# Moving the gate products ahead of the pair products in an RWKV-5 attention that feeds a mixture of experts

## The chip, the core and the metric

The kernel runs on one core of a Trainium2 chip. The metric is device time in microseconds (us) of one execution of the whole program, attention and experts together. A core has five engines that run on their own and wait for each other through semaphores: TensorE (PE in the profile; PEld is its row of weight loads, which overlap the products), VectorE (DVE), ScalarE (ACT), GpSimd (POOL) and SyncE (SP, which here only issues transfers).

## The reference, cut to what matters

```
batch, n_heads, seq, head_dim = (4, 8, 768, 48)
for t in range(S):
    kt, vt, rt = (k[:, :, t], v[:, :, t], r[:, :, t])
    cur = np.einsum('bhd,bhe->bhde', u[None] * kt, vt)
    y[:, :, t] = np.einsum('bhd,bhde->bhe', rt, state + cur)
    state = w[None, :, :, None] * state + np.einsum('bhd,bhe->bhde', kt, vt)
...
logits = x @ w_gate          # x: y as 3072 rows (tokens) of 384
# each token goes to one of 8 experts, best logits first, at most 384 tokens to an expert
h = np.maximum(x[mask] @ w1[e], 0.0)
out[mask] = h @ w2[e]
```

The gate's product, `x @ w_gate`, is what the change moves. The logits decide which tokens an expert takes, and the experts' two products come after that.

## The kernel before

The attention is class `Mild`. It cuts the sequence into 24 units of 128 steps of one batch: unit n is chunk n // 4 of batch n % 4 (N = 24, B = 4, C = 6). The order of all instructions is written out by hand, and each engine takes its own in that order. `run` makes one round for each unit, in a software pipeline: in round n, unit n + 2 is turned (transposed), unit n + 1 gets its pair products, and unit n its outputs. On TensorE a round from n = 3 on is this:

- `turn(n + 2)`: four transposes of the keys into `kT_ps` and four of the receptances into `rT_ps` (L458).
- `rows((n - 1,), "few")` (L685): four transposes of the finished unit n - 1 into `x_ps` (L595). ScalarE copies that out to `xr` (L604), and SP sends it to the token table in memory. This stands in rounds 1 to 20.
- `keep(n - 1)` (L695), in rounds up to n = 4 only: the state's products into `kv_ps` (L524).
- `pairs(n + 1)` (L697): 16 products of 48 rows into `g_ps` (L505). VectorE then copies the lower triangle from `g_ps` into `AT` with a mask, in two instructions (L512).
- In a round with a gate only, `gate(n // B - 1, ...)` (L705): 16 products into `lg_ps` (L575), four for each of four units n - 4 to n - 1, with the weights `wgp`. ScalarE copies them to `lg` (L580). These rounds are n = 4, 8, 12, 16 and 20 (`full`); a sixth gate comes after the last round and is not touched.
- `outputs(n)` (L711): eight products from the states (L545, `y_ps<-rT,states`), the eight of `keep(n)` (L524), and eight from `AT` (L545, `y_ps<-AT,vts`). After a gate a transpose of `lg` into `lt_ps` ends the round (L585), which ScalarE copies to the logits `LG` (L586). ScalarE then copies `y_ps` to `x` (L564).

What matters around the change is the buffer of the `few` tag. `x_ps` (L591), `lg_ps` (L571) and `lt_ps` (L584) all come from it, and its pool has one buffer. So a gate's first product waits until ScalarE's copy at L604 has read the `x_ps` before it. The `wgp` of the gate comes by two transfers that SP issues in round 2 (L404). `g_ps` has one buffer too, which VectorE's masked copy of the round before must have read.

ScalarE's share of a gate round is: the copy of `kT_ps` (L475), `xr` (L604), four diagonals of `AT` (L495), `lg` (L580), four more diagonals, `LG` (L586) and `x` (L564). VectorE's is: `rT` (L477), the masked copies (L512), and the state's sum (L529), beside the tables and the early steps of the assignment. In rounds 17 to 23 the assignment of an early expert is woven in (L1152 to L1270, products L1167, L1203, L1218).

After round 23 the last logits go into the assignment search, on VectorE for the most part, while TensorE runs the early expert. Then the eight experts follow, for which TensorE is busy nearly without a break.

Of the kernel before, what the change touches and what calls it, by code (L numbers as in the profile page):

```python
# [274 lines left out]
class Mild:  # L275
# [343 lines left out]
    def run(self, step):  # L619
        N, B, C, walk = self.N, self.B, self.C, self.walk  # L620
        self.live = {n: {} for n in range(N)}
        self.start()
        u_ps = self.spread_u()
        self.again_one(0, 0)
        k0 = self.keys_turned(0, True)
        self.again_one(0, 1)
        self.idle(2, "g_ps")
        r0 = self.r_turned(0)
        self.copy_u(u_ps)
        self.own(0)  # L630
        self.scaled(0, "k", k0, "pieces")
        self.scaled(0, "r", r0, "pieces")
        self.table(self.WK, "k")
        self.again_one(1, 0)
        self.table(self.WR, "r")
        self.again_one(1, 1)
        self.idle(2, "g_ps")
        k1 = self.keys_turned(1, True, walk.ps, "few")
        wk_ps = self.wk_turned()
        r1 = self.r_turned(1, walk.ps, "counts")  # L640
        self.wk_table(wk_ps)
        self.scaled(1, "k", k1, self.WK)
        self.own_sum(0)
        self.diagonal(0, (0,))
        self.again_one(2, 0)
        self.diagonal(0, (1,))
        self.again_one(2, 1)
        self.scaled(1, "r", r1, self.WR)
        self.own(1)
        self.keys(0)  # L650
        self.own_sum(1)
        nc, AB = self.nc, self.ones8
        nc.vector.tensor_mul(self.chunk, AB[:, 0, :, 1, 8], AB[:, 0, :, 1, 8])
        self.pairs(0)
        self.diagonal(1)
        self.own(2)
        chores = walk.constants()
        for n in range(N):
            self.load(n + 5, "kr")
            self.load(n + 4, "v")  # L660
            if n == 2:
                self.gate_weights()
            soon, split, full = n <= B, 0 < n < 3, n >= B and n % B == 0
            halves = ((0,), (1,)) if split or full else ((0, 1), ())
            if n == 0:
                self.turn(2, True)
                self.own_sum(2)
                self.idle(3, "y_ps")
                self.pairs(1)
                self.keys(1)  # L670
            else:
                step(n, "first")
                if not soon and n + 3 < N:
                    self.again(n + 3)
                if n == 2:
                    self.own_sum(n + 2)
                if split:
                    self.keep(n - 1)
                    self.pairs(n + 1)
                if n + 2 < N:  # L680
                    if n != 2 and n + 3 < N:
                        self.own_sum(n + 2)
                    self.turn(n + 2, between=lambda: step(n, "turning"))
                if n <= N - B:
                    self.rows((n - 1,), "few")  # L685
            if soon:
                self.again_one(n + 3, 0)
            if n + 2 < N:
                self.diagonal(n + 2, halves[0])
            if soon:  # L690
                self.again_one(n + 3, 1)
            if n > 2:
                step(n, "turned")
                if n <= B:
                    self.keep(n - 1)  # L695
                if n + 1 < N:
                    self.pairs(n + 1, lambda: step(n, "products"))  # L697
                step(n, "paired")
            if n + 3 < N:
                self.keys(n + 3)  # L700
                self.own(n + 3)
                if n == 1:
                    self.keys(2)
            if full:
                self.gate(n // B - 1, range(B))  # L705
                if n + 2 < N:
                    self.diagonal(n + 2, halves[1])
            if n == N - 1:
                rows = self.rows_turned((N - 4, N - 3), "g_ps", lambda: step(n, "rows"))
                self.rows_out((N - 4, N - 3), rows)  # L710
            self.outputs(n, lambda: step(n, "states"), (lambda: self.logits(n // B - 1)) if full else (lambda: None))  # L711
            if split:
                self.diagonal(n + 2, halves[1])
            if n == N - 4:
                self.own_sum(N - 1)
            step(n, "last")
            if n == 13:
                walk.guess_most(self.LG[:, 0:3 * B, :], AX.XY)
            if n == 14:
                walk.guess(walk.ps.tile([128, 128], F32, name="most_ps", tag="few"), self.ident)  # L720
            if n == N // 2 + 1:
                for _ in chores:
                    pass
                self.test()
            if n > 2:
                for _ in range(6):
                    next(chores, None)
        self.gate(C - 1, range(B - 1))
        one = self.rows_turned((N - 2,), "kT_ps")
        self.gate(C - 1, [B - 1])  # L730
        last = self.rows_turned((N - 1,), "g_ps")
        self.logits(C - 1)
        return one, last
# [1285 lines left out]
```

## Time and profile before

| | us |
|---|---|
| median of 3 runs | 393.32 (393.11 to 393.7) |
| the profiled execution's own time | 393.36 |
| its span, first to last instruction | 391.6 |
| rounds 4 to 20 in it, about | 30 to 113 |
| last logits copied, the search begins, about | 126.8 |

Times in the rows are us from the span's start. A row of the timeline gives start, length, engine, source line, operation, output<-inputs, shape and count, and in brackets how long the engine was idle before it and what ended that; "issue" there means that no wait which the profile shows did. TensorE's fp32 products appear twice each, so the 16 of a gate read x32. The span is 1.8 us shorter than that execution's time, and the execution lies within 0.04 us of the median.

### The profile page before, as it was taken

What the parts mean: (1) busy time and instruction counts of PE and PEld (TensorE: products, weight loads), DVE (VectorE), ACT (ScalarE), POOL (GpSimd) and SP (SyncE); (2) the same over time, 40 slices, a digit from 0 to 9 for tenths busy, and PEclk for the clock granted to TensorE, in tenths of its full rate; (3) what the DMA queues carried; (4) which work ended last, traced back from release to release, by engine and by line L of the source; (5) the groups of instructions that cost most, each with busy time, mean ns of one, the idle gap of its engine ahead of it and who ended that gap; (6) DMA issues with size and microseconds to landing.
All of it is one profiled execution on the core that took longest, in us unless ns stands there. A gap on an engine that the chain in (4) does not pass through costs nothing. (4 is left out here: it accounts for less than half of the span.)

```text
span 391.6 us, 9858 instructions
## 1 busy us (share of the span) xinstructions
PE 377.2 (96%) x3777; PEld 306.2 (78%) x3777; DVE 281.4 (72%) x959; ACT 169.3 (43%) x452; POOL 141.2 (36%) x173
## 2 busy tenths in 40 slices
PE   8899999999999999999999999999999999999992
PEld 7677888888877866687578899558657889989991
DVE  6755777586885788985949949888378976994530
ACT  4997989888883311312222242121222234234220
POOL 7878887767732022032122021203203212070020
PEclk9999999999999999999999999999999999999997
DMA  9999999988692164651560560109209264280010
GB/s 121 160 180 174 210 189 201 174 171 157 129 338 82 43 241 181 195 190 42 164 238 28 168 251 20 41 5 345 77 20 338 85 231 173 52 329 24 2 62 27
DMA packets 95335, 57.35 MB, mean 146 GB/s; under 512 B 77232, under 2 KB 89520, under 8 KB 95280
## 3 DMA queue, kind: packets, MB, share of 16 engines
q1 hardware_dynamic: 91936, 47.21, 48.0%
q0 software_dynamic: 3104, 9.44, 7.0%
q8 instruction: 31, 0.51, 0.6%
q14 instruction: 24, 0.20, 0.2%
q10 hardware_dynamic: 240, 0.00, 0.0%
HBM read 47.20 MB, written 9.44 MB: 145 GB/s over the span
## 5 line engine op out<-in xcount | busy, mean ns | idle before, releaser
L1624 PE MATMUL h_ps<-xT,w 128*128 128x384 f32 (+1 forms) x264 | 72.6, 427 | 0.0
L495 ACT ACTIVATE AT<-ident,dd 128x128 f32<-128x128 f32 x192 | 59.6, 392 | 2.2 <-DVE dd L448 2.1
L1624 PEld LDWEIGHTS h_ps<-xT,w 128*128 128x128 f32 x264 | 42.0, 191 | 19.6 <-issue 2.2
L1518 POOL DMA_INDIRECT xg<-x_rows,tok x22 | 22.5, 1021 | 92.4 <-PE h_ps L1624 23.7
L1750 POOL DMA_INDIRECT out_dram<-o_all,to x16 | 20.8, 1299 | 85.3 <-DVE o_all L1738 22.2
L1627 ACT ACTIVATE hid<-h_ps 128x384 f32<-128x384 f32 (+1 forms) x40 | 17.9, 449 | 54.2 <-PE h_ps L1624 50.9
L512 DVE COPY_PREDICATED AT<-mask,g_ps 64x512 f32<-64x512 uint8 (+1 forms) x48 | 32.4, 723 | 11.7 <-PE g_ps L505 9.9
L1756 PE MATMUL o_ps<-w,hid 128*128 128x384 f32 x96 | 32.5, 490 | 0.0
L505 PE MATMUL g_ps<-rT,kT 48*64 48x128 f32 (+1 forms) x768 | 26.3, 255 | 1.8 <-DVE AT L512 1.0
L436 POOL TENSOR_TENSOR kss<-krs,wk 128x384 f32<-128x384 f32 x24 | 24.3, 1016 | 8.0 <-DVE krs L340 5.0
L1756 PEld LDWEIGHTS o_ps<-w,hid 128*128 128x128 f32 x96 | 17.7, 190 | 10.6 <-issue 0.5
L545 PE MATMUL y_ps<-AT,vts 128*64 128x128 f32 x384 | 25.7, 276 | 0.0
L443 POOL TENSOR_TENSOR rk<-rk,u_bc 128x384 f32<-128x384 f32 x24 | 24.1, 1003 | 1.9
L505 PEld LDWEIGHTS g_ps<-rT,kT 48*64 48x64 f32 x768 | 20.6, 132 | 5.1 <-PE unread_ps L418 0.9
L442 POOL TENSOR_TENSOR rk<-krs 128x384 f32<-128x384 f32 x24 | 24.5, 1022 | 0.2 <-DMA krs<-in_r_dram 0.2
L545 PEld LDWEIGHTS y_ps<-AT,vts 128*64 128x64 f32 x384 | 20.6, 137 | 1.0 <-issue 0.7
L477 DVE TENSOR_TENSOR rT<-rT_ps,WR 112x512 f32<-112x512 f32 x23 | 15.7, 683 | 4.2 <-PE rT_ps L458 4.2
L448 DVE TENSOR_REDUCE dd<-rk 128x8 f32<-128x384 f32 x24 | 13.1, 545 | 6.9 <-POOL rk L443 6.9
L564 ACT COPY x<-y_ps 128x512 f32<-128x512 f32 x24 | 14.1, 586 | 5.9 <-PE y_ps L545 5.0
L458 PE MATMUL rT_ps<-ident,krs 128*112 128x128 f32 x96 | 15.4, 281 | 0.5 <-DMA krs<-in_r_dram 0.4
L1698 PE MATMUL pa_ps<-T,S 128*128 128x192 f32 x80 | 15.8, 331 | 0.0
L1729 PE MATMUL p_ps<-W,H 128*128 128x128 f32 x128 | 15.8, 275 | 0.0
(340 smaller groups left out, 834.2 us busy)
## 6 DMA issues: line engine op xcount, KB each, us to landing
w<-in_moe_w_dram SPq DMA_DIRECT2D x18, 1536.0 KB, 8.7
krs<-in_k_dram SPq DMA_DIRECT2D x24, 192.0 KB, 4.5
krs<-in_r_dram SPq DMA_DIRECT2D x24, 192.0 KB, 4.8
vts<-in_v_dram SPq DMA_DIRECT2D x24, 192.0 KB, 4.9
x_rows<-xr SPq DMA_DIRECT2D x24, 192.0 KB, 3.5
xg<-x_rows,tok POOLq DMA_INDIRECT x22, 4.0
out_dram<-o_all,to POOLq DMA_INDIRECT x16, 2.7
out_dram<-o_sb,to POOLq DMA_INDIRECT x5, 4.7
```

The costliest lines, as they stand in the source:

```text
L436: self.nc.gpsimd.tensor_mul(self.kss[:, n % self.NS].rearrange("p (g h) d -> p g h d", g=2)[:, :, :, 0:D], src, self.wk.rearrange("p (g h) ...
L442: nc.gpsimd.tensor_mul(rk, self.krs[:, n % self.NK, 1, 0:H, 0:D], self.krs[:, n % self.NK, 0, 0:H, 0:D])
L443: nc.gpsimd.tensor_mul(rk, rk, self.u_bc)
L495: nc.scalar.mul(AT[:, z, a, :], self.ident, dd[:, h:h + 1])
L505: nc.tensor.matmul(g_ps[ts(i, PD), z, a, i * PD:], kT[rows, a, ts(i, PD)], rT[rows, a, i * PD:], start=True, stop=True)
L512: nc.vector.copy_predicated(out=AT[keys, :, :, steps], mask=mask, data=g_ps[keys, :, :, steps])
L545: nc.tensor.matmul(yv[q * PD:(q + 1) * PD, o // 2, o % 2, :], lhsT, rhs, start=(o // 2, q) not in seen, stop=stop, skip_group_check=True)
L1518: nc.gpsimd.indirect_dma_start(out=xg[:, c, :], out_offset=None, in_=x_dram[0:within, :], in_offset=bass.IndirectOffsetOnAxis(ap=tok[:, c: ...
L1624: nc.tensor.matmul(h_ps[j][:, at], w1[:, f, ts(j, 128)], xT[:, f, at], start=(f == 0), stop=(f == KD - 1))
L1627: nc.scalar.activation(hid[:, j, 0:m], h_ps[j][:, 0:m], AF.Relu)
L1750: nc.gpsimd.indirect_dma_start(out=to, out_offset=bass.IndirectOffsetOnAxis(ap=tok, axis=0), in_=o_sb, in_offset=None)
L1756: nc.tensor.matmul(o_ps, hid[:, j, ts(c, 128)], w2[:, j, :], start=(j == 0), stop=(j == KF - 1))
```

## The change

```diff
@@ -693,6 +693,10 @@
                 step(n, "turned")
                 if n <= B:
                     self.keep(n - 1)
+                if full:
+                    self.gate(n // B - 1, range(B))
+                    if n + 2 < N:
+                        self.diagonal(n + 2, halves[1])
                 if n + 1 < N:
                     self.pairs(n + 1, lambda: step(n, "products"))
                 step(n, "paired")
@@ -701,10 +705,6 @@
                 self.own(n + 3)
                 if n == 1:
                     self.keys(2)
-            if full:
-                self.gate(n // B - 1, range(B))
-                if n + 2 < N:
-                    self.diagonal(n + 2, halves[1])
             if n == N - 1:
                 rows = self.rows_turned((N - 4, N - 3), "g_ps", lambda: step(n, "rows"))
                 self.rows_out((N - 4, N - 3), rows)
```

In the five rounds with a gate its 16 products stand ahead of the 16 pair products. The copy of `lg` and the four diagonals move along in the source. But no instruction of `pairs`, `keys` or `own` that they pass runs on ScalarE, so ScalarE's queue keeps its order; so do the queues of VectorE, GpSimd and SP. Only TensorE's order changes.

The rows below are TensorE's queue in round 8, before. `x_ps` is the turned unit 7, `g_ps` the pair products, `lg_ps` the gate; `x_765` and so on are the units' buffers, and a bracket names the queues whose semaphores a row waits for.

```order
L595 MATMUL x_ps<-ident,x_1053 128x112 x3
L505 MATMUL g_ps<-rT,kT 64x128 [waits DVE_49,PE_49]
L505 MATMUL g_ps<-rT,kT 64x64
...
L575 MATMUL lg_ps<-x_765,wgp 32x128 [waits Activation_49]
L575 MATMUL lg_ps<-x_861,wgp 32x128
...
L545 MATMUL y_ps<-rT,states 64x128 x8
L524 MATMUL kv_ps<-vts,kss 64x48 [waits DMAHW6_49,DVE_49]
```

With the change the same place reads as follows.

```order
L595 MATMUL x_ps<-ident,x_1053 128x112 x3
L575 MATMUL lg_ps<-x_765,wgp 32x128 [waits Activation_49]
L575 MATMUL lg_ps<-x_861,wgp 32x128
...
L505 MATMUL g_ps<-rT,kT 64x128 [waits DVE_49]
L505 MATMUL g_ps<-rT,kT 64x64
...
L545 MATMUL y_ps<-rT,states 64x128 x8
L524 MATMUL kv_ps<-vts,kss 64x48 [waits DMAHW6_49,DVE_49]
```

The gate now follows the transposes into `x_ps` directly, and the pair products come directly ahead of the products from the states. Rounds 12, 16 and 20 are moved alike.

In round 4, TensorE's queue has the state's products of `keep(3)` behind `x_ps`, and the gate waits for the two transfers of its weights as well. Before:

```order
L524 MATMUL kv_ps<-vts,kss 64x48 x7
L505 MATMUL g_ps<-rT,kT 64x128 [waits DVE_49,PE_49]
L505 MATMUL g_ps<-rT,kT 64x64
...
L575 MATMUL lg_ps<-x_387,wgp 32x128 [waits DMAHW6_49,DMAHW5_49,Activation_49]
L575 MATMUL lg_ps<-x_466,wgp 32x128
...
L545 MATMUL y_ps<-rT,states 64x128 x8
```

With the change:

```order
L524 MATMUL kv_ps<-vts,kss 64x48 x7
L575 MATMUL lg_ps<-x_387,wgp 32x128 [waits DMAHW6_49,DMAHW5_49,Activation_49]
L575 MATMUL lg_ps<-x_466,wgp 32x128
...
L505 MATMUL g_ps<-rT,kT 64x128 [waits DVE_49]
L505 MATMUL g_ps<-rT,kT 64x64
...
L545 MATMUL y_ps<-rT,states 64x128 x8
```

Here the wait for the transfers moves from behind the pair products to ahead of them.

## The prediction

> **What bounds the kernel now.** I read the page first, then the waits of TensorE's weight loads in the attention, then the timeline of each engine around the five rounds with a gate, and last the place where the attention hands over to the search.
>
> ```profile
> PE 377.2 (96%) x3777; PEld 306.2 (78%) x3777; DVE 281.4 (72%) x959; ACT 169.3 (43%) x452; POOL 141.2 (36%) x173
> ```
>
> Products overlap, so 96% is no proof. The waits are: this is all that the weight loads waited for in the stretch from 40 to 70 us, longest groups first, with total, times and the longest one.
>
> ```profile
> PEld kv_ps L524 <- issue: 1.0, 6, 0.2
> PEld kT_ps L458 <- issue: 1.0, 6, 0.2
> ...
> PEld lg_ps L575 <- issue: 0.2, 1, 0.2
> ```
>
> No engine is waited for by more than 0.2 us; the gaps are 0.2 us each, at fixed places in a round. TensorE bounds the attention, by the length of its queue. Behind the attention VectorE stands ready and waits 3.56 us for the last logits:
>
> ```profile
> 126.85 0.35 DVE L1030 TENSOR_REDUCE m<-LG 128x24 f32<-128x192 f32 x1 [3.56 <-ACT LG L586]
> ```
>
> The search, the tokens' lists and the experts all hang on that row. What TensorE loses or wins by then, the end loses or wins, unless a later round has slack. That gives the method: for each gate round, when does the first product behind the moved block start, before and after?
>
> **The change part by part.** Nothing is added or removed; 16 gate products and 16 pair products change places, five times. Round 8 before, on the weight loads' row:
>
> ```profile
> 50.96 0.45 PEld L595 LDWEIGHTS x_ps<-ident,x 112*128 112x128 f32 x4
> 51.54 0.85 PEld L505 LDWEIGHTS g_ps<-rT,kT 48*64 48x64 f32 x32
> 52.57 0.81 PEld L575 LDWEIGHTS lg_ps<-x,wgp 128*32 128x32 f32 x32 [0.17 <-issue]
> 53.58 0.43 PEld L545 LDWEIGHTS y_ps<-rT,states 48*64 48x64 f32 x16 [0.20 <-issue]
> 54.18 0.55 PEld L524 LDWEIGHTS kv_ps<-vts,kss 128*64 128x64 f32 x16 [0.17 <-DVE AT L512]
> ```
>
> From the pair products' start to that of `kv_ps` it takes 54.18 - 51.54 = 2.64 us, of which the gate, with the gap behind it, is 53.58 - 52.57 = 1.01. A round without a gate has the order that pair products and states get with the change, one right behind the other:
>
> ```profile
> 42.83 0.84 PEld L505 LDWEIGHTS g_ps<-rT,kT 48*64 48x64 f32 x31
> 43.54 0.14 PEld L545 LDWEIGHTS y_ps<-rT,states 48*64 48x64 f32 x2
> ...
> 44.29 0.55 PEld L524 LDWEIGHTS kv_ps<-vts,kss 128*64 128x64 f32 x16 [0.17 <-issue]
> ```
>
> Here both take 44.29 - 42.83 = 1.46 us, and there is no gap between them: the states' loads begin before the last pair product's. So the new order takes 1.01 + 1.46 = 2.47 us where the old took 2.64. **Term one** is a gain of 0.17 us a round: one gap less.
>
> The Trainium skill says of these gaps (TensorEngine Tiling (Array Packing), Key Properties) that changing the tiling mode, not merely the tile, drains TensorE. The rows agree: the gap stands where 48*64 meets 128*32, and none where 48*64 follows 48*64. By that rule alone the change is a gain of one drain a round; by the rows it is also a wait, which follows.
>
> **Term two** is that wait. The gate's output lies in the one buffer from which ScalarE must first copy `x_ps`. These are ScalarE's copies in rounds 8, 12 and 16, and for 12 and 16 the pair products' start, which is where the gate would now stand.
>
> ```profile
> 51.65 0.48 ACT L604 COPY xr<-x_ps 128x384 f32<-128x384 f32 x1 [0.18 <-PE x_ps L595]
> 70.47 0.48 ACT L604 COPY xr<-x_ps 128x384 f32<-128x384 f32 x1 [0.18 <-PE x_ps L595]
> 89.74 0.48 ACT L604 COPY xr<-x_ps 128x384 f32<-128x384 f32 x1 [0.18 <-PE x_ps L595]
> ```
>
> ```profile
> 70.36 0.85 PEld L505 LDWEIGHTS g_ps<-rT,kT 48*64 48x64 f32 x32
> ...
> 89.63 0.86 PEld L505 LDWEIGHTS g_ps<-rT,kT 48*64 48x64 f32 x32
> ```
>
> How soon TensorE goes on after ScalarE shows once in round 4:
>
> ```profile
> 30.77 0.59 ACT L564 COPY x<-y_ps 128x512 f32<-128x512 f32 x1
> ...
> 31.41 0.39 PEld L595 LDWEIGHTS x_ps<-ident,x 112*128 112x128 f32 x4 [0.35 <-ACT x L564]
> ```
>
> The copy ends at 31.36 and TensorE starts 0.05 us later. So in round 8 the gate can start at 51.65 + 0.48 + 0.05 = 52.18, instead of at 51.54 when TensorE is free: 0.64 us in which TensorE's whole queue stands. In round 12 it is 71.00 against 70.36, in round 16 90.27 against 89.63: 0.64 each. Before, the pair products lay over that copy and it cost nothing. Net of term one, each of the three rounds loses 0.64 - 0.17 = 0.47 us, 1.41 together. The bounds for one: 0.17 gained if TensorE somehow need not wait, 0.64 lost if the gap does not go.
>
> **Round 4** has other neighbours: the state's products stand between `x_ps` and the moved block, and the gate's weights are just arriving.
>
> ```profile
> 31.95 0.55 PEld L524 LDWEIGHTS kv_ps<-vts,kss 128*64 128x64 f32 x16
> 32.55 0.86 PEld L505 LDWEIGHTS g_ps<-rT,kT 48*64 48x64 f32 x32
> 33.72 0.84 PEld L575 LDWEIGHTS lg_ps<-x,wgp 128*32 128x32 f32 x32 [0.31 <-issue]
> 34.76 0.42 PEld L545 LDWEIGHTS y_ps<-rT,states 48*64 48x64 f32 x16 [0.20 <-issue]
> 35.35 0.55 PEld L524 LDWEIGHTS kv_ps<-vts,kss 128*64 128x64 f32 x16 [0.17 <-DVE AT L512]
> ```
>
> ```profile
> 32.05 0.48 ACT L604 COPY xr<-x_ps 128x384 f32<-128x384 f32 x1 [0.21 <-PE x_ps L595]
> ```
>
> ```profile
> L404 SPq DMA_DIRECT2D wgp<-in_moe_w_gate_dram x2: 434/623/812, 28.4 to 29.3; - x2
> DMA to landing us min/median/max: 4.3/4.7/5.0
> ```
>
> ```profile
> L575 PEldq EVENT_SEMAPHORE  x1: 51/51/51, 33.6 to 33.6; - x1
> ```
>
> ScalarE's copy is over at 32.53, so it costs nothing here. But the second transfer of the weights is issued at 29.3 and cannot land before 29.3 + 4.3 = 33.6, and TensorE's wait for it was passed at 33.6: already before, the gate started at the moment its weights came. SP's queue is not changed, so the gate again starts at 33.72, while TensorE is free at 32.55. The pair products then start 1.04 later (33.72 to 34.76) at 34.76, and `kv_ps` 1.46 behind them at 36.22, against 35.35: 0.87 us lost. The bounds: if the weights were there in time, the gate would start at 32.58 and `kv_ps` at 32.58 + 1.04 + 1.46 = 35.08, 0.27 gained. I take 0.87, since the trace has the very transfer.
>
> **Round 20** has slack behind it.
>
> ```profile
> 109.17 0.88 PEld L505 LDWEIGHTS g_ps<-rT,kT 48*64 48x64 f32 x32 [0.23 <-PE x_ps L595]
> ...
> 112.86 0.14 PEld L585 LDWEIGHTS lt_ps<-ident,lg 128*128 128x128 f32 x1 [0.17 <-issue]
> ...
> 113.76 0.15 PEld L1203 LDWEIGHTS <-e_row 128*128 128x128 f16 x3 [0.31 <-issue]
> ...
> 116.04 0.10 PEld L1167 LDWEIGHTS <-ones 128*128 128x128 bf16 x1 [0.32 <-DVE e_acc L1163]
> ```
>
> ```profile
> 109.18 0.48 ACT L604 COPY xr<-x_ps 128x384 f32<-128x384 f32 x1 [0.18 <-PE x_ps L595]
> ...
> 113.54 0.17 ACT L586 COPY LG<-lt_ps 128x32 f32<-128x32 f32 x1
> ```
>
> ```profile
> 114.06 0.55 DVE L448 TENSOR_REDUCE dd<-rk 128x8 f32<-128x384 f32 x1 [1.20 <-POOL rk L443]
> ```
>
> By the same sum the gate starts at 109.18 + 0.48 + 0.05 = 109.71, 0.54 late, and `lt_ps` comes 0.54 - 0.17 = 0.37 late, at 113.23. ScalarE's copy of it began at 113.54 before, so it is late by 0.37 at the most. The product at 113.76 writes the same buffer and waits for that copy, 0.31 before, and the one at 116.04 waits for VectorE, which itself waited 1.20 us for GpSimd; neither of those two hangs on TensorE's round 20. So the loss of 0.37 is gone at 116.04. I take 0; the bounds are 0 and 0.37.
>
> **What else is late.** The masked copy starts with the pair products, so it moves by 0.64 + 1.01 = 1.65 us:
>
> ```profile
> 52.78 1.36 DVE L512 COPY_PREDICATED AT<-mask,g_ps 64x512 f32<-64x512 uint8 x2 [0.36 <-PE g_ps L505]
> ...
> 56.91 0.69 DVE L477 TENSOR_TENSOR rT<-rT_ps,WR 112x512 f32<-112x512 f32 x1 [0.29 <-PE rT_ps L458]
> ```
>
> In round 8 it now ends at 52.78 + 1.36 + 1.65 = 55.79. Its readers are the outputs of round 9, and `g_ps` is overwritten by the pair products of round 9, both behind the 12 transposes that open that round. VectorE's next TensorE-bound step waited 0.29 at 56.91, so VectorE may run some tenths late into round 9, where `rT` is not read before round 10. I cost this at nothing; it is covered by a round's length.
>
> **The sum.** 0.87 + 3 x 0.47 + 0 = 2.28 us. The profiled execution took 393.36 with its span of 391.6, and the median is 393.32, so either base gives the same: 393.36 + 2.28 = **395.6 us**. A measurement of this kernel can tell about 0.2%, that is 0.79 us, from no change; the sum is nearly three times that.
>
> **The rivals.**
>
> *The gap decides, not the wait.* If the gate did not wait for ScalarE (its loads and products running on while `x_ps` is copied out), only term one is left, in all five rounds: 5 x 0.17 = 0.85 us faster, 392.5. That is where the Trainium skill's drain rule, taken alone, leads. It would decide if the wait were below 0.17 us a round; by the rows it is 0.64, and round 4's transfer would have to land a microsecond sooner as well. The queue's listing has the gate wait for ScalarE, and one buffer leaves no other way. Chance 0.05.
>
> *The weights come in time.* If in most executions the second transfer lands before 32.5, round 4 gains 0.27 instead of losing 0.87: 393.36 + 1.41 - 0.27 = 394.5. For it: the two landings differ by 0.7 us already. Against it: the wait was passed at just the landing. Chance 0.12.
>
> *The late rounds give back.* Behind round 20 TensorE waits 0.31 at 113.76, 0.32 at 116.04 and 0.90 ahead of the last pair products:
>
> ```profile
> 117.93 0.68 PEld L505 LDWEIGHTS g_ps<-rT,kT 48*64 48x64 f32 x27 [0.90 <-ACT x L564]
> ```
>
> Less a gap of 0.17 each, that is 1.02 us that TensorE could make up, if those waits ended at times of their own: 395.6 - 1.0 = 394.6. Against it: VectorE's early steps begin from a product of TensorE in round 19, so they shift with it, and what ends these waits shifts too. Chance 0.10. Together with the rival before, 2.28 - 1.14 - 1.02 leaves 0.1 us: 393.5, no change that can be measured. Chance 0.06.
>
> *Round 20 pays too.* If GpSimd or VectorE there are held up by the later pair products, its 0.37 is carried: 396.0. For it: in the stretch from 108 to 113 us VectorE (third busy time) works 4.82 of 5.00 us.
>
> ```profile
> 108.00:113.00 5.00, 4.95 (x108) 4.05 (x107) 4.82 (x11) 3.42 (x11) 2.45 (x3) 1.00 1.05 399
> ```
>
> Against it stands the wait for GpSimd right behind that stretch. Chance 0.12.
>
> My forecast has the remaining 0.55. The range runs from 394.3, a little under the second and third rivals, to 396.3, a little over the last; it leaves out the first rival and the no-change case, and some of the spread at the edges. Faster by over 0.2% is the first rival alone, 0.05; within 0.2% the case of no change, 0.06; slower all the rest, 0.89.
>
> **What the profile after should show.** The rows of round 8 in the order `x_ps`, `lg_ps`, `g_ps`, `y_ps`, with TensorE idle by about 0.6 us ahead of `lg_ps` and that put down to ScalarE's L604, again in rounds 12 and 16; in round 4 some 1.1 us ahead of `lg_ps`, with the weights' semaphore passed at 33.6 as before; no gap between pair products and states; and the distance from gate to gate longer by 0.47. The step from round 4's `kv_ps` to round 16's should grow by 1.41, the last logits should be copied 2.3 us later, and the rest should follow unchanged. I would be wrong if the gate started at 51.54 on its heels, if round 4's wait ended much before 33.6, or if the logits' copy came later but the end did not.

## The result, and the profile after

| | before | with the change |
|---|---|---|
| median us | 393.59 (393.11 to 393.7, 7 runs) | 395.82 (394.9 to 397.56, 7 runs) |
| ratio | | 1.0067, 95% interval 1.0046 to 1.0089 |
| span of the profiled execution | 391.6 | 394.1 |

The change makes the kernel slower by 0.67%, some 2.6 us by the ratio and 2.2 by the medians. The forecast was 395.6, within 394.3 to 396.3.

These are the weight loads of round 8 with the change, in the columns of the timeline shown before.

```profile
51.99 0.39 PEld L595 LDWEIGHTS x_ps<-ident,x 112*128 112x128 f32 x4
53.16 0.81 PEld L575 LDWEIGHTS lg_ps<-x,wgp 128*32 128x32 f32 x32 [0.78 <-ACT xr L604]
54.17 0.84 PEld L505 LDWEIGHTS g_ps<-rT,kT 48*64 48x64 f32 x31 [0.20 <-issue]
54.88 0.14 PEld L545 LDWEIGHTS y_ps<-rT,states 48*64 48x64 f32 x2
...
55.63 0.55 PEld L524 LDWEIGHTS kv_ps<-vts,kss 128*64 128x64 f32 x16 [0.17 <-issue]
```

The gate waits 0.78 us, and the profile names ScalarE's copy L604 as what ended it. Some 0.13 of that is no loss: before, TensorE stood idle that long between `x_ps` and the pair products (50.96 + 0.45 = 51.41 to 51.54). Gate to pair products is 54.17 - 53.16 = 1.01, pair products to `kv_ps` 55.63 - 54.17 = 1.46, and the states' loads begin without a gap. ScalarE in the same round:

```profile
52.63 0.48 ACT L604 COPY xr<-x_ps 128x384 f32<-128x384 f32 x1 [0.21 <-PE x_ps L595]
53.11 1.28 ACT L495 ACTIVATE AT<-ident,dd 128x128 f32<-128x128 f32 x4
54.31 0.27 ACT L580 COPY lg<-lg_ps 128x128 f32<-128x128 f32 x1
```

The copy ends at 53.11 and the gate starts 0.05 us later. The copy of `lg`, which had waited 0.41 us for the gate before, now follows ScalarE's diagonals without a wait. That is what the new order gives ScalarE, and nothing needs it.

Rounds 12, 16 and 20 repeat the wait:

```profile
72.46 0.81 PEld L575 LDWEIGHTS lg_ps<-x,wgp 128*32 128x32 f32 x32 [0.78 <-ACT xr L604]
...
92.21 0.81 PEld L575 LDWEIGHTS lg_ps<-x,wgp 128*32 128x32 f32 x32 [0.78 <-ACT xr L604]
...
112.14 0.81 PEld L575 LDWEIGHTS lg_ps<-x,wgp 128*32 128x32 f32 x32 [0.78 <-ACT xr L604]
```

And round 4:

```profile
32.26 0.55 PEld L524 LDWEIGHTS kv_ps<-vts,kss 128*64 128x64 f32 x16
33.79 0.84 PEld L575 LDWEIGHTS lg_ps<-x,wgp 128*32 128x32 f32 x32 [0.99 <-ACT krs L344]
34.83 0.84 PEld L505 LDWEIGHTS g_ps<-rT,kT 48*64 48x64 f32 x31 [0.20 <-issue]
...
36.30 0.55 PEld L524 LDWEIGHTS kv_ps<-vts,kss 128*64 128x64 f32 x16 [0.17 <-issue]
```

The name behind that arrow misleads. L344 copies into the keys' buffer, which the gate does not read. The products' own row has the real cause, the weights' landing, and the semaphore is passed at 33.7:

```profile
L575 PEldq EVENT_SEMAPHORE  x1: 51/51/51, 33.7 to 33.7; - x1
its engine sat idle before it (us, times) until:
  ACT krs L344: 1.0, 1
  DMA wgp<-in_moe_w_gate_dram: 0.9, 1
```

Last, round 20 and the hand-over:

```profile
110.10 0.40 PEld L458 LDWEIGHTS kT_ps<-ident,kss 128*112 128x112 f32 x4 [0.17 <-issue]
...
118.46 0.10 PEld L1167 LDWEIGHTS <-ones 128*128 128x128 bf16 x1 [0.26 <-DVE e_acc L1163]
```

```profile
129.27 0.35 DVE L1030 TENSOR_REDUCE m<-LG 128x24 f32<-128x192 f32 x1 [3.56 <-ACT LG L586]
```

The search begins at 129.27 instead of 126.85, 2.42 us late, with the same wait of 3.56 ahead of it. The end is 2.5 late.

Measured from one round's first load into `kT_ps` to the next round's, the rounds with a gate are as long as this:

| round | before | with the change | difference |
|---|---|---|---|
| 4 | 6.95 | 7.58 | +0.63 |
| 8 | 5.59 | 6.10 | +0.51 |
| 12 | 5.59 | 6.07 | +0.48 |
| 16 | 5.59 | 6.07 | +0.48 |
| 20 | 5.24 | 5.60 | +0.36 |

The first four make 2.10. Another 0.32 was there when round 4 began (its first load at 30.27 instead of 29.95), and 2.10 and 0.32 make the 2.42 at the hand-over. The 0.32 comes from TensorE's loads near the start, ahead of any instruction that the change moves. Up to 8.14 us the loads of the two executions start at the same times. Then follow, before and with the change:

```profile
8.84 0.47 PEld L427 LDWEIGHTS wk_ps<-ident,WK 128*128 128x128 f32 x4
```

```profile
9.00 0.87 PEld L427 LDWEIGHTS wk_ps<-ident,WK 128*128 128x128 f32 x4
```

The same four loads took nearly twice as long with the change, at a granted clock of 1.00 in both. It does not hang on the change: e11 below, the same kernel, has 0.47 there. Of the thirteen traces, the six in which these loads took 0.61 to 0.87 us begin round 4 at 30.25 to 30.31, and the seven with 0.47 at 29.71 to 30.00. Why the loads stay slow for longer in some executions is open.

### The profile page after: what moved, and what is told of

Same layout as the page of the kernel before. It is cut to its first block, busy times and chain, and to the rows that moved or that the text cites. A ratio compares the mean times of both kernels' runs of the same rounds, so it can differ in the third digit from the quotient of the medians.

```text
span 394.1 us, 9853 instructions
## 1 busy us (share of the span) xinstructions
PE 377.2 (96%) x3777; PEld 306.9 (78%) x3777; DVE 281.5 (71%) x959; ACT 168.8 (43%) x452; POOL 141.0 (36%) x173
## 5 line engine op out<-in xcount | busy, mean ns | idle before, releaser
L545 PE MATMUL y_ps<-rT,states 48*64 48x128 f32 x320 | 16.0, 276 | 0.0
```

The source lines that it names most:

```text
L545: nc.tensor.matmul(yv[q * PD:(q + 1) * PD, o // 2, o % 2, :], lhsT, rhs, start=(o // 2, q) not in seen, stop=stop, skip_group_check=True)
```

## The experiments

The theory was that the whole loss is two waits, the gate's for ScalarE's copy of `x_ps` and, in round 4, for its weights, less one gap of 0.17 us a round. The rival was that the order itself costs, through late pair products and a late masked copy. Eleven runs were made in three groups, each group on one chip and compared with before on that chip. On the chip of the second group before took 394.56 us, against 393.58 and 393.69 on the others, so ratios are compared, and differences in us are worked out from the ratio.

| run | ratio to before, 95% interval | us |
|---|---|---|
| e1 own bank for the gate | 1.0015 (1.0006 to 1.0024) | +0.6 |
| e2 weights sooner | 1.0037 (1.0024 to 1.0050) | +1.5 |
| e3 both | 1.0002 (0.9993 to 1.0011) | +0.1 |
| e4 both, in the old order | 0.9998 (0.9989 to 1.0007) | -0.1 |
| e5 round 4 alone | 1.0020 (1.0011 to 1.0029) | +0.8 |
| e6 rounds 8, 12, 16 alone | 1.0039 (1.0026 to 1.0053) | +1.5 |
| e7 round 20 alone | 1.0002 (0.9992 to 1.0012) | +0.1 |
| e8 e3 without its new wait | 0.9995 (0.9983 to 1.0007) | -0.2 |
| e9 gate behind the states' products | 0.9984 (0.9975 to 0.9993) | -0.6 |
| e10 ScalarE's copy made twice | 1.0092 (1.0076 to 1.0109) | +3.6 |
| e11 the change again | 1.0058 (1.0041 to 1.0075) | +2.3 |

**e1, a bank of its own.** On top of the change:

```diff
-            self.lgs[c] = self.walk.ps.tile([128, T], F32, name="lg_ps", tag="few")
+            self.lgs[c] = self.walk.ps.tile([128, T], F32, name="lg_ps", tag="few" if c == 0 else "counts")
```

> The changed order, but in rounds 8, 12, 16 and 20 the gate's output lies in the state products' bank (tag counts) instead of the bank of x_ps; round 4 as in the change. My theory (the loss is the gate's wait for ScalarE's copy of x_ps, and round 4's wait for its weights): no idle ahead of lg_ps in rounds 8, 12, 16, 20 beyond the usual 0.17 or so; from pair products to kv_ps 1.46 and for gate and pairs together 2.47, so each round gains 0.17 against before; round 4 loses its 0.6 to 0.9 as in the change. Sum against before: 0.65 to 0.9 less 3 x 0.17 = +0.1 to +0.4 us, 393.7 to 394.0. Rival (the order itself costs, because the pair products and VectorE's masked copy come late): it stays at +1.5 or more, and TensorE waits somewhere behind the pair products.

The loads of its round 8, and of its round 20:

```profile
51.54 0.40 PEld L595 LDWEIGHTS x_ps<-ident,x 112*128 112x128 f32 x4
52.07 0.81 PEld L575 LDWEIGHTS lg_ps<-x,wgp 128*32 128x32 f32 x32
53.08 0.84 PEld L505 LDWEIGHTS g_ps<-rT,kT 48*64 48x64 f32 x31 [0.20 <-issue]
...
54.55 0.55 PEld L524 LDWEIGHTS kv_ps<-vts,kss 128*64 128x64 f32 x16 [0.17 <-issue]
```

```profile
110.52 0.81 PEld L575 LDWEIGHTS lg_ps<-x,wgp 128*32 128x32 f32 x32 [1.53 <-DVE states L529]
```

The wait for ScalarE is gone from rounds 8, 12 and 16, and these are now shorter than before by 0.12, 0.16 and 0.16 us: the gap. So the order itself costs nothing. But the expectation overlooked that the new bank is read by VectorE (L529), which in round 20 is late with the early expert's steps. There a new wait of 1.53 us took the place of the old one, and that round became 1.11 us longer than before. Round 4 lost only 0.19 where 0.6 to 0.9 was expected: its weights came sooner, and the gate started at 33.34. In the time +0.6 (0.2 to 0.9) was measured where +0.1 to +0.4 was expected. The search begins at 127.24, 0.39 later than before, but 0.31 of that was there when round 4 began; the rest of the time is taken up under e11.

**e2, the weights sooner.** On top of the change:

```diff
-            if n == 2:
+            if n == 1:
                 self.gate_weights()
```

> The changed order, with the two transfers of the gate's weights issued in round 1 instead of round 2. My theory: the semaphore of the weights has long been passed in round 4, the gate starts as soon as kv_ps is through, and round 4 gains 0.17 to 0.27 against before instead of losing 0.64; rounds 8, 12 and 16 lose 0.47 to 0.51 each as in the change. Sum +1.1 to +1.4, 394.7 to 395.0, about 1 us under the change. Rival (round 4's loss was made good later, or came from elsewhere): no difference from the change, +2.2.

```profile
31.92 0.55 PEld L524 LDWEIGHTS kv_ps<-vts,kss 128*64 128x64 f32 x16
32.56 0.81 PEld L575 LDWEIGHTS lg_ps<-x,wgp 128*32 128x32 f32 x32
...
35.04 0.55 PEld L524 LDWEIGHTS kv_ps<-vts,kss 128*64 128x64 f32 x16 [0.17 <-issue]
```

In round 4 the gate starts right behind `kv_ps`, and the round takes 6.67 us, 0.28 less than before, against 7.58 with the change: the round's loss is the wait for the weights and nothing else. Rounds 8, 12 and 16 still lose 0.54, 0.48 and 0.48. The sum by rounds is +1.2 and the time +1.5 (0.9 to 2.0).

**e3, both edits.** 

> Both together: own bank for the gate from round 8 on, and the weights in round 1. My theory: nothing but the gap is left of the change, 0.17 gained in rounds 8, 12 and 16 and 0.2 to 0.3 in round 4, round 20 hidden: -0.7 to -0.8 us against before, about 392.8, faster than both kernels. Rival (order itself costs): +0.5 or more.

The rounds gain what was said: -0.28, -0.12, -0.16, -0.16, together 0.72 us. In round 20, however, the wait of 1.53 us for VectorE stands as in e1. The search begins at 126.52, only 0.33 sooner than before, so about half of the gain is spent on the bank that I had chosen. In time nothing is left of it that can be told from no change (-0.3 to +0.4). Where the other half went in the profiled execution, its trace shows: into waits for transfers. Two gathers of tokens took some 0.06 each (`xg`, at 127.1 and 149.8), and a step of VectorE waited for an expert's weights. Before, and in e3:

```profile
300.26 0.69 DVE L1673 TENSOR_TENSOR W<-w 128x512 f32<-128x512 f32 x1 [1.23 <-DMA w<-in_moe_w_dram]
```

```profile
300.25 0.76 DVE L1673 TENSOR_TENSOR W<-w 128x512 f32<-128x512 f32 x1 [1.44 <-DMA w<-in_moe_w_dram]
```

TensorE then waits 0.26 us for VectorE at 302.39, and at 303.65 it is no longer ahead of before (303.63). Whether its other executions lose the gain at the same place is not shown.

**e4, both edits in the old order.** 

> The order of before with the same two edits (own bank, weights in round 1), so that the order alone stands against e3. My theory: in the old order neither wait cost anything but 0.14 us in round 4, so -0.1 us against before or no change, 393.3 to 393.6; e3 is 0.5 to 0.7 under it. Rival (the edits themselves bring what e3 brings): e4 as fast as e3.

No change, as expected; but e3 is not the 0.5 to 0.7 under it that was expected too. The bank costs something in the old order as well: in round 20 the gate waits 0.42 us for VectorE, and the round is 0.25 longer than before. By rounds the order does what was said: rounds 8, 12 and 16 take 5.59 us each here, as before, and 5.46, 5.43 and 5.43 in e3.

**e5, e6 and e7, the rounds apart.** Each has the new order in some rounds only, and the old one, `if full and not (...)`, in the others.

```diff
-                if full:
+                if full and n == 4:             # e5;  4 < n < 20 in e6;  n == 20 in e7
                     self.gate(n // B - 1, range(B))
```

> Only round 4 has the new order. My theory (the gate there is tied to the landing of its weights, at 33.6 to 33.7 us, whatever TensorE does): kv_ps of round 4 starts 0.6 to 0.9 us later than before, and the end follows: 394.1 to 394.5. Rival (made good later): no change, 393.6.

> Only rounds 8, 12 and 16 have the new order. My theory: each is 0.47 to 0.51 us longer (0.64 to 0.68 of waiting for ScalarE's copy of x_ps, less 0.17 for one gap), all carried to the end: +1.4 to +1.5, 395.0 to 395.1. Rival (the waits are taken up in rounds 17 to 23, where TensorE waits for VectorE): +0.4 to +1.0.

> Only round 20 has the new order. My theory: its lt_ps comes 0.35 us late, but the product at the early expert's e_acc in round 21 starts no later than before, since VectorE ends that wait: no change at the end, 393.4 to 393.8. Rival (round 20 is carried too): +0.37, 394.0.

e6 came as expected: its three rounds are longer by 0.48 us each, 1.44 together, and the time by 1.5 (1.0 to 2.1). In e7 round 20 is longer by 0.36 and the end does not move. Its rows show why, from round 20's first load to the product that waits for VectorE:

```profile
107.47 0.40 PEld L458 LDWEIGHTS kT_ps<-ident,kss 128*112 128x112 f32 x4 [0.17 <-issue]
...
115.81 0.10 PEld L1171 LDWEIGHTS <-ones 128*128 128x128 bf16 x1 [0.25 <-DVE e_acc L1167]
```

That distance is 8.34 us, against 8.37 before. In the interval, +0.37 is not excluded by the time alone (-0.3 to +0.5); the rows decide. e5 took +0.8 (0.4 to 1.1) in time. In its profiled execution, though, the weights came sooner (the gate at 33.49, idle 0.69) and round 4 was longer by 0.32 us only. One execution is one landing. By the time, e5, e6 and e7 add up to 2.4, close to the change's 2.3 to 2.6.

**e10, the copy made twice.** On top of the change, in rounds 8, 12 and 16 a second copy of `x_ps` by ScalarE:

```diff
+            if len(ns) == 1 and n in (7, 11, 15):
+                nc.scalar.copy(xr, ps[:, i].rearrange("p o (z d) -> p (o z) d", z=2)[:, :, 0:D])
             nc.scalar.copy(xr, ps[:, i].rearrange("p o (z d) -> p (o z) d", z=2)[:, :, 0:D])
```

> The change, with ScalarE copying x_ps to xr twice in rounds 8, 12 and 16, so that the buffer comes free one copy later (about 0.38 to 0.48 us, as two copies run 0.38 apart elsewhere). My theory: the idle time ahead of lg_ps grows from 0.78 to 1.16 to 1.26 in these three rounds and the end moves by 1.1 to 1.4 us more: +3.5 to +4 against before. Rival (the gate does not hang on that copy): no more than the change, +2.2 to +2.6.

```profile
53.53 0.81 PEld L575 LDWEIGHTS lg_ps<-x,wgp 128*32 128x32 f32 x32 [1.29 <-ACT xr L606]
```

```profile
52.48 0.48 ACT L605 COPY xr<-x_ps 128x384 f32<-128x384 f32 x1 [0.21 <-PE x_ps L595]
53.00 0.48 ACT L606 COPY xr<-x_ps 128x384 f32<-128x384 f32 x1
```

The second copy starts 0.52 us behind the first (both write the same tile), a little later than I had taken, and the wait grows by just that, 0.78 to 1.29. Three times 0.51 is 1.5; the time is 3.6 us over before, and 1.3 over e11's 2.3. The gate hangs on that copy.

**e11, the change again.** 

> The change as it is, beside the others on one chip. My theory: +2.1 to +2.6 us against before, with the same waits ahead of lg_ps: 0.78 in rounds 8, 12, 16 and 20, and in round 4 whatever the landing of the weights sets. Rival (its runs, from 394.9 to 397.6, hold a second effect beyond the waits): a spread again three times that of before.

+2.3 us (1.6 to 3.0), with 0.78 us of waiting in rounds 8, 12, 16 and 20, and 1.07 in round 4, where this execution began 0.3 sooner than the one profiled first. The spread is wide again, 394.67 to 396.93 against 393.09 to 394.0 of before. The chain that ended last shows one cause. It runs through the last write but one. Its row in the profiled executions of before, and of e11:

```profile
377.23 2.62 DMA out_dram<-o_all,to
```

```profile
379.55 4.73 DMA out_dram<-o_all,to
```

The very last write, of `o_last`, stands behind a branch in the kernel's text. Here is ScalarE's copy of its rows and then its issue, first before and then in e11:

```profile
384.79 0.48 ACT L1758 COPY o_last<-o_ps 128x384 f32<-128x384 f32 x1 [4.88 <-PE o_ps L1756]
...
385.71 0.97 POOL L1750 DMA_INDIRECT out_dram<-o_last,tok_last  x1 [7.51 <-ACTq L1973]
```

```profile
387.11 0.48 ACT L1758 COPY o_last<-o_ps 128x384 f32<-128x384 f32 x1 [4.88 <-PE o_ps L1756]
...
389.25 0.97 POOL L1750 DMA_INDIRECT out_dram<-o_last,tok_last  x1 [8.72 <-issue]
```

The write before it took 2.6 to 2.9 us in six of the profiled executions (before, the change, e3, e5, e9, e10), and there the last issue follows the end of the copy by 0.43 or 0.44 us. It took 3.6 in e4 and 4.0 to 4.7 in the six others (e1, e2, e6, e7, e8, e11). There the issue follows the copy by 0.5 to 1.7 us, and the landing of the long write by 4.95 to 5.13. So the end waits for the later of the two, and a long write adds 0.1 to 1.2 us. In e11's profiled execution ScalarE's copy is 2.32 late and the issue 3.54. In e1's the copy is 0.48 late and the issue 1.19. This blurs differences below a microsecond. Why the write is long in some executions, and whether a given order makes that more frequent, was not tried, so how much of the measured time it makes up is open.

**e8, e3 without its new wait.** The changed order in rounds 4 to 16 only, the gate's own bank in rounds 8, 12 and 16, the weights in round 1.

```diff
-                if full:
+                if full and n < 20:
                     self.gate(n // B - 1, range(B))
...
-name="lg_ps", tag="few")
+name="lg_ps", tag="counts" if c in (1, 2, 3) else "few")
```

> The changed order in rounds 4, 8, 12 and 16, the old one in round 20; the gate's own bank only in rounds 8, 12 and 16; the weights' transfers in round 1. It takes out of e3 the wait for VectorE that e3 met in round 20 (1.53 us ahead of lg_ps). My theory: only the gap is left, -0.28 in round 4 and -0.12 to -0.16 in each of the three others: -0.7 against before. Rival (e3's missing gain lay elsewhere): no change, as e3.

By rounds it gains what was expected, -0.28, -0.10, -0.16, -0.16, 0.70 together, and no wait is left ahead of a gate. The search begins at 125.94, 0.91 sooner than before (0.21 of it was there when round 4 began). The gain lasts through all the experts: ScalarE's copy of the last rows starts at 383.82, against 384.79 before, which is 0.97 sooner. Yet that execution's span, 391.8, is no shorter than before's. It has the long write, 4.54 us, and the last write is issued at 385.87, against 385.71. In time e8 is at -0.2 (-0.7 to +0.3), so the gain is seen up to the last product and is not shown in the time.

**e9, the gate behind the states' products.** The pair products stay where they were before, and the gate goes back by one place instead of forward.

```diff
-            if full:
-                self.gate(n // B - 1, range(B))
-                if n + 2 < N:
-                    self.diagonal(n + 2, halves[1])
+            def gated():
+                if full:
+                    self.gate(n // B - 1, range(B))
+                    if n + 2 < N:
+                        self.diagonal(n + 2, halves[1])
...
+        gated()          # in outputs, behind the products from the states
         if c > 0:
             self.keep(n)
```

> The pair products stay ahead as before, and the gate goes one step back instead: behind the products from the states, ahead of keep(n). ScalarE's order is unchanged. My theory: pair products and states then stand side by side as in the change (one gap of 0.17 less a round), and ScalarE's copy and the weights' transfer are long over when the gate comes, so nothing is paid: 0.17 each gained in rounds 8, 12 and 16, 0.2 to 0.3 in round 4, round 20 hidden: -0.7 us, about 392.8, the fastest of all. Rival (the gap is not tied to the neighbours, or the late gate delays the copy of lg and with it lt_ps at the round's end): no gain, 393.5 or more.

```profile
51.56 0.84 PEld L505 LDWEIGHTS g_ps<-rT,kT 48*64 48x64 f32 x31
52.28 0.14 PEld L545 LDWEIGHTS y_ps<-rT,states 48*64 48x64 f32 x2
...
53.03 0.81 PEld L576 LDWEIGHTS lg_ps<-x,wgp 128*32 128x32 f32 x32 [0.17 <-issue]
54.04 0.55 PEld L524 LDWEIGHTS kv_ps<-vts,kss 128*64 128x64 f32 x16 [0.20 <-issue]
```

Pair products and states' products stand side by side, and ahead of the gate only the usual gap is left. Rounds 8, 12 and 16 are shorter than before by 0.16 us each and round 4 by 0.33 (the weights are there in time too). The time is 0.6 us under before (0.3 to 1.0), the only version that is faster beyond its interval. Its trace bears that out against e7's from the same chip: round 4 begins 0.41 later in e9 (30.31 against 29.90) and the search 0.24 sooner (127.05 against 127.29).

## Why the prediction was right

*TensorE bounds the attention, and its loss is carried to the end.* Right for a loss: 2.42 us at the hand-over, 2.5 at the end. A gain is not always carried: e3's was gone at 304 us.

*Term one, one gap less, 0.17 us.* Right. Pair products to `kv_ps` is 1.46 us, as taken from a round without a gate. Where the wait is taken away (e1, e3, e8) or never met (e9), what is left is a gain of 0.16 a round, of 0.10 to 0.12 in round 8 of e1, e3 and e8. The Trainium skill's rule (TensorEngine Tiling (Array Packing), Key Properties), that a change of tiling mode drains TensorE, agrees with these rows: the gap goes where 48*64 follows 48*64.

*Term two, 0.64 us of waiting for ScalarE in rounds 8, 12 and 16.* Right, with 0.47 net against 0.51, 0.48 and 0.48 measured. The 0.04 more in round 8 come ahead of `x_ps`, whose transposes started a little late on ScalarE's copy of `x`. e6 measures the term alone, e10 doubles its cause, e1 removes it.

*Round 4, 0.87.* The mechanism was right, the size too large in every execution profiled: 0.63 with the change, 0.72 in e11, 0.49 in e10, 0.32 in e5 and 0.19 in e1. The gate starts some 0.1 us behind the semaphore of its weights (33.79 behind 33.7 with the change, 33.61 behind 33.5 in e11, 33.49 behind 33.4 in e5), while TensorE comes there by its own pace. The sum held both fixed, as they were in one trace. The landing moves, though: the gate starts at 33.34 to 33.79 in these five. So does TensorE's arrival: round 4 begins at 30.00 to 30.27, against 29.95. Before's own 6.95 us hold 0.14 of waiting as well; e6 and e7, with the old order in round 4, took 6.78 and 6.80. e2 shows that nothing but this landing is behind the loss.

*Round 20, 0.37 and then nothing.* Right: 0.36, gone at the product that waits for VectorE, in the change (118.46 - 110.10 = 8.36 us, against 8.37) and in e7.

*The masked copy at no cost.* Right by e1, e3 and e8: with the copy still late by the gate's 1.01 us, rounds 8 to 16 are shorter than before.

*The sum.* 2.28 was forecast, and the time moved by 2.2 to 2.6. The mechanism carries most of that, but so close a hit is luck in part. The rounds made 2.10, since round 4 gave less than its term, and 0.32 of the profiled difference is none of the change's. The interval of the time alone runs from 1.8 to 3.5 us, and TensorE's start, the landing of the weights and the write at the end each move single executions by several tenths. Of the rivals, the first (the gap alone decides) falls with the wait that is in every trace. The second (the weights in time) was made true in e2, and round 4 then gave 0.28 where the rival said 0.27. The third (late rounds give back) is excluded because round 21's product and the hand-over are both 2.42 late, and the fourth (round 20 pays) by the 8.36 against 8.37.

## What to carry to other kernels

When two blocks on the bounding engine are exchanged, ask of each what the other was covering: here the pair products lay over a copy of 0.48 us and the landing of a transfer, and the gate had nothing to put in their place. If the gain is a neighbourhood (two blocks with one tiling side by side), look for a second order that makes the same neighbours without uncovering anything: moving the gate back by one place (e9) gave the gap and paid nothing. And a buffer lent from elsewhere to remove a wait brings its own last reader along; in e1 and e3 that was VectorE at its busiest.

## What the runs showed of the hardware

A change of tiling costs TensorE's weight loads 0.17 us nearly wherever it stands in these rounds, and 0.20 on leaving 128*32; behind `x_ps` it is 0.13. The four loads into `wk_ps`, at about 9 us, took anything from 0.47 to 0.87 us at a granted clock of 1.00, and the executions with the slow ones began round 4 some 0.3 us later. The last write but one took anything from 2.6 to 4.7 us, and the end waits for it when it is long; before single executions are compared within 1 us, both rows have to be looked at. The second group's chip ran before 1 us slower, and in all four profiles from it VectorE's wait ahead of the search is 4.2 us instead of 3.56; before itself was not traced there, so the cause stays open.
